# Loading the first two chunks of a windowed-attention kernel from two DMA queues instead of one

## Chip, cores and metric

The kernel runs on one core of a Trainium2 chip. The metric is the device time of one execution in microseconds (us). The kernel before took 175.13 and 176.15 us in two runs, with a median of 175.64 us. A lower time is better.

## What is computed

The input is four batches of eight heads, 768 tokens each, with 64 values per head. Each query sees the 128 tokens up to and including itself and, beyond these, the first four tokens of its batch (the sinks). The attention output goes through a feed-forward network with three first-layer matrices, of whose products the elementwise maximum is taken. The reference, cut to its core:

```python
scores = scale * np.matmul(q, k.transpose(0, 1, 3, 2))
is_sink = pos[None, :] < 4
rel = pos[:, None] - pos[None, :]
keep = is_sink | ((rel >= 0) & (rel < 128))
a = softmax(np.where(keep, scores, -1e9))
x = np.matmul(a, v)                      # to tokens x 512
h = np.maximum(np.maximum(x @ w1, x @ w2), x @ w3)
out = h @ w_out                          # 3072 x 512, float32
```

## The kernel before

**Tiling.** The 3072 tokens are cut into twelve chunks of 256 tokens (`ci` 0 to 11, three to a batch). For each chunk `load` (L93) brings Q, K and V of all eight heads from HBM as float32 tiles of 128 partitions by 8 heads by 2 tokens by 64 values, 512 KB each. With `parts=2` a load is cut by heads into two pieces of 256 KB: `part=0` holds heads 0 to 3 and `part=1` heads 4 to 7. An argument `gate` makes a small GpSimd instruction write into the tile first, so that the load waits for GpSimd; `eng` names the engine that issues the load, and is SyncE when it is left out.

**Stages of a chunk.** `cast_qk` (L112) turns half of the heads (`g` 0 or 1) of Q or K into bfloat16. `turn` (L132) and `turn2` (L156) transpose such a half with four TensorE matmuls against an identity into a PSUM tile `pt`, and copy that to `qT` or `kT`. `premask` (L306) writes an additive mask into the score tiles `st` with a matmul against the identity, `score` (L314) adds the products of `qT` and `kT` for the head pairs that it is given, `expo` (L392) takes the exponential on ScalarE into `e_sb`. Head half `g=1` serves pairs 2 and 3, half `g=0` pairs 0 and 1. `cast_v` (L121) turns V into bfloat16; `av` (L460) multiplies the probabilities with it into the tile `o`; `norm` (L478) divides, with a reciprocal and a multiplication on VectorE, into `x_sb`. `xpose` (L490) transposes `x_sb`, `ffn_h` (L511, matmuls on L524) makes the first layer with its maximum, `ffn_y` (L545) the second, `store` (L604) writes the result.

**The order of the work.** The schedule is written out by hand: each engine works through its instructions in the order in which the program text issues them to it, and waits only on semaphores for the data of others. Lines 191 to 265 set up constants; here ScalarE loads its activation table for the exponential (L194, by a first activation `one`), and VectorE zeroes the tile `wz`. From L639 on stands the start of the pipeline, call by call. `warm` (L198) issues matmuls of zeros whose result nobody reads: eight on L640 and four more on L650, between the transposes of Q's first half and the first mask. Since TensorE takes its instructions in order, whatever stands behind a warm call waits for it.

**Queues.** Before, every load of Q, K and V is issued by SyncE (SP), in the order: Q of chunk 0, heads 4 to 7 (L639); all of K (L641); Q, heads 0 to 3 (L642); V in two halves (L643, L645), the first of them gated by a GpSimd memset (L619); then K, Q and V of chunk 1 (L655, L663, L670). In the pages the transfers that SP or ScalarE issues are "hardware_dynamic" and show under one queue number. The weights are issued by GpSimd (`load_w`, L289), as "software_dynamic", each behind a cast on that engine that waits for an input: w1's columns 512 to 768 behind the cast of V of chunk 0, the next piece behind the cast of K of chunk 1, the third behind that of Q of chunk 1.

Of the kernel before, what the change touches and what calls it, by code (L numbers as in the profile page):

```python
# [16 lines left out]
def kernel(  # L17
# [13 lines left out]
    nc = tc.nc  # L31
# [17 lines left out]
    with tc.manual_schedule():  # L49
# [7 lines left out]
        def bank(shape, dtype, name):  # L57
            j = free.pop(0)
            x = psum.tile(shape, dtype, tag=f"b{j}", name=name)
            home[id(x)] = x, j  # L60
            return x
# [31 lines left out]
        def load(ci, what="kqv", gate=None, part=None, parts=1, eng=None):  # L93
            if ci >= NCH:
                return
            b, c = divmod(ci, CPB)
            t0 = c * 256
            for w in what:
                src = {"k": k, "q": q, "v": v}[w]
                if (ci, w) not in raws:  # L100
                    raws[ci, w] = raw.tile([128, H, 2, D], F32, tag=w + "_raw", name=w + "_raw")
                dst = raws[ci, w]
                if gate is not None:
                    gate(dst[0:1, 0, 0, 0:1])
                n = H // parts
                for g in range(parts) if part is None else (part,):
                    (eng or nc.sync).dma_start(
                        out=dst[:, n * g:n * g + n],
                        in_=src[b, n * g:n * g + n, t0:t0 + 256]
                            .rearrange("h (p i) d -> p h (i d)", i=2))  # L110

        def cast_qk(ci, w, g, eng):  # L112

            if (ci, w) not in bfs:
                bfs[ci, w] = raw.tile([128, NP, 2, 2, D], BF16, tag=w + "_bf", name=w + "_bf")
            x, y = bfs[ci, w], raws[ci, w]
            f = eng.copy if eng is nc.scalar else eng.tensor_copy
            f(x[:, 2 * g:2 * g + 2].rearrange("q p i a d -> q p a i d"),  # L118
              y[:, 4 * g:4 * g + 4].rearrange("q (p a) i d -> q p a i d", a=2))
# [12 lines left out]
        def turn(ci, w, g, eng=None):  # L132

            pt = bank([128, 4, 128], BF16, "pt")
            x = bfs[ci, w]
            for i in range(4):
                y = x[:, 2 * g + i // 2, i % 2]
                nc.tensor.transpose(pt[:, i], y.rearrange("s a d -> s (a d)"), ident)  # L138
            eng = eng or (nc.scalar if w == "q" else nc.vector)
            f = eng.copy if eng is nc.scalar else eng.tensor_copy  # L140
            if w == "q":
                f(
                    qT[ci % RING][:, 2 * g:2 * g + 2].rearrange("q p i n r -> q (p i) (n r)"), pt)
            elif ci >= NEW:
                f(
                    keys(ci)[:, 2 * g:2 * g + 2].rearrange("q p n h (i r) -> q p i (n h) r", i=2),
                    pt.rearrange("q (p i) (j r) -> q p i j r", p=2, j=4))
            else:
                f(
                    kT[ci % RING][:, :, 2 * g:2 * g + 2].rearrange("q n p i r -> q n (p i) r"),  # L150
                    pt.rearrange("q x (n r) -> q n x r", r=64))
            give(pt)
# [37 lines left out]

        wz = const.tile([128, 512], BF16, name="wz")
        nc.vector.memset(wz, 0.0)
        one = const.tile([128, 1], F32, name="one")
        nc.scalar.activation(one, wz[:, 0:1], AF.Exp)  # L194
        for x in vb:
# [2 lines left out]
        def warm(n):  # L198

            if n:  # L200
                pw = bank([128, 512], F32, "warm")
                for _ in range(n):
                    nc.tensor.matmul(pw, lhsT=wz[:, 0:128], rhs=wz, start=True, stop=True)  # L203
                give(pw)
# [14 lines left out]
        def masks():  # L219
            nc.gpsimd.memset(addm[:, 0:2], 0.0)  # L220
            for i in range(2):
                hp = slice(64 * i, 64 * i + 64)
                nc.gpsimd.affine_select(
                    out=addm[hp, 1], in_=addm[hp, 1], compare_op=ALU.is_ge, fill=NEG,
                    base=-i, pattern=[[1, 2], [2, 64]], channel_multiplier=-2)
                nc.gpsimd.affine_select(
                    out=addm[hp, 0], in_=addm[hp, 0], compare_op=ALU.is_gt, fill=NEG,
                    base=i, pattern=[[-1, 2], [-2, 64]], channel_multiplier=2)
            nc.vector.tensor_copy(addm0[:, 0], addm[:, 1])
            nc.vector.tensor_copy(addm0[:, 1], addm[:, 0])  # L230
            nc.vector.tensor_copy(addm0[:, 2], addm[:, 1])
            for i in range(2):
                nc.vector.memset(addm0[64 * i:64 * i + 2, 0:2], 0.0)
            nc.vector.tensor_copy(addm[:, 2:4], addm[:, 0:2])
# [71 lines left out]
        def premask(ci, pairs):  # L306
            lo = 0 if ci % CPB else 1
            for p in pairs:
                sts[ci, p] = [bank([128, 4, 128], F32, "st") for a in range(2)]
                for a in range(2):  # L310
                    nc.tensor.matmul(sts[ci, p][a][:, lo:], lhsT=ident, rhs=addm0 if lo else addm,  # L311
                                     start=True, stop=False, skip_group_check=True)
# [79 lines left out]
        def expo(ci, p):  # L392
            if ci >= NEW:
                return expo4(ci, p)
            lo = 0 if ci % CPB else 1
            e, st = es[ci, p]
            for a in range(2):
                nc.scalar.activation(e[:, a, lo:], st[a][:, lo:], AF.Exp, scale=scale)  # L398
                give(st[a])
# [238 lines left out]

        load(0, 'q', part=1, parts=2)  # L639
        warm(8)  # L640
        load(0, 'k')  # L641
        load(0, 'q', part=0, parts=2)  # L642
        load(0, 'v', part=0, parts=2, gate=pool_gate)  # L643
        cast_qk(0, 'q', 1, nc.scalar)
        load(0, 'v', part=1, parts=2)  # L645
        masks()
        sink_init()
        factors(msk, addm)
        turn(0, 'q', 1, nc.scalar)
        warm(4)  # L650
        premask(0, (2,))
        cast_qk(0, 'k', 0, nc.scalar)
        cast_qk(0, 'k', 1, nc.vector)
        turn(0, 'k', 1, nc.vector)
        load(1, 'k')  # L655
        turn(0, 'k', 0, nc.scalar)
# [3 lines left out]
        score(0, (3,))  # L660
        turn(0, 'q', 0, nc.vector)
        premask(0, (0,))
        load(1, 'q')  # L663
        expo(0, 2)
        cast_v(0, 1, 0, nc.gpsimd)
        cast_v(0, 0, 0, nc.vector)
# [333 lines left out]
```

## Time and profile before

| what | value |
|---|---|
| runs | 175.13 and 176.15 us, median 175.64 us |
| span of the profiled execution, first to last instruction | 173.5 us |
| median less that span | 2.14 us |
| TensorE busy, share of the span | 167.7 us, 97% |
| VectorE, ScalarE, GpSimd busy | 125.1, 88.8, 110.1 us |
| chain that ended last, by engine | TensorE 93%, VectorE 3%, ScalarE 1% |
| moved by DMA | 35.22 MB, mean 203 GB/s |

The profile is of one execution. Of that execution the page gives the span; what lies around it (start and end of the program) is taken as the difference to the median of the runs, 2.14 us. Engines are named PE (TensorE), PEld (its weight loads), DVE (VectorE), ACT (ScalarE), POOL (GpSimd) and SP (SyncE); a name with a q behind it is that engine's DMA queue. A row of the timeline holds the start and the duration in us, the engine, the line, the operation, what it writes and reads, and in brackets how long the engine had been idle and what released it. A row of the chain holds start, length and what stood in the chain.

### The profile page before, as it was taken

To read this page: it belongs to the slowest core of one execution; us is meant where nothing else is said; L and a number is where in the kernel's file an instruction comes from. 1 tells how busy PE (TensorE), PEld (TensorE's weight loads), DVE (VectorE), ACT (ScalarE), POOL (GpSimd) and SP (SyncE) were. 2 spreads that over 40 slices of the span, in tenths; PEclk is the share of its full clock that TensorE was granted. 3 is DMA by queue.
4 is the path that set the end of the run, shared out by engine and by line. 5 is a ranking of instruction groups with operands and counts; after the bars stand their busy time and mean duration, and the time that the engine had idled before them with its cause. 6 is when DMAs were issued, how large, how long until landed. Compare 5 with 4: busy or idle time off the path is not lost.

```text
span 173.5 us, 5418 instructions
## 1 busy us (share of the span) xinstructions
PE 167.7 (97%) x2225; PEld 129.2 (74%) x2225; DVE 125.1 (72%) x262; ACT 88.8 (51%) x183; POOL 110.1 (63%) x193
## 2 busy tenths in 40 slices
PE   7979999999999999999999999999999999999992
PEld 2546889857695697797797797797897896896871
DVE  3187856696697985986877977877778876776361
ACT  4598554587944615817726717627636516510210
POOL 7389507445399999999999999999998700000000
PEclk9999999999999999999999999999999999999999
DMA  4999999999996999988999969969999119017303
GB/s 134 300 289 198 216 217 252 219 274 290 292 210 118 250 264 180 252 188 220 264 186 247 264 165 254 257 163 238 257 176 274 32 34 376 21 35 272 121 2 121
DMA packets 71545, 35.22 MB, mean 203 GB/s; under 512 B 27488, under 2 KB 69984, under 8 KB 71520
## 3 DMA queue, kind: packets, MB, share of 16 engines
q1 hardware_dynamic: 65824, 31.60, 79.0%
q0 software_dynamic: 5552, 3.15, 12.8%
q8 instruction: 17, 0.28, 0.7%
q10 hardware_dynamic: 144, 0.13, 0.2%
q14 instruction: 8, 0.07, 0.1%
HBM read 25.17 MB, written 6.29 MB: 181 GB/s over the span
## 4 chain that ended last, share of the span: by engine, by line
PE 93%; DVE 3%; ACT 1%; issue 0%
PE h_ps L524 55%; PE y_ps L577 11%; PE y_ps L553 7%; PE o L471 7%; PE st L357 3%; PE warm L203 3%; PE st L331 3%; PE pt L138 2%; ACT e_sb L398 1%; PE o L453 1%; DVE x_sb L484 1%; PE sk L423 1%; PE y_ps L599 1%; DVE vb L123 1%; PE xt L496 1%; PE st L311 0%
## 5 line engine op out<-in xcount | busy, mean ns | idle before, releaser
L524 PE MATMUL h_ps<-xT,w 128*128 128x256 bf16 x864 | 101.2, 273 | 0.1
L524 PEld LDWEIGHTS <-w 128*128 128x128 bf16 x864 | 81.9, 98 | 9.9 <-issue 0.3
L540 DVE TENSOR_TENSOR h_sb<-h_sb,h_ps 128x512 bf16<-128x512 bf16 (+1 forms) x74 | 49.3, 671 | 20.0 <-PE h_ps L524 16.0
L536 ACT CAST h_sb<-h_ps 128x512 bf16<-128x512 f32 x35 | 20.5, 585 | 52.2 <-PE h_ps L524 52.2
L129 POOL CAST vb<-v_raw 32x512 bf16<-32x512 f32 x48 | 36.7, 764 | 2.8 <-DMA v_raw<-in_v_dram 0.6
L90 POOL CAST k_bf<-k_raw 32x512 bf16<-32x512 f32 x48 | 29.5, 614 | 2.2
L398 ACT ACTIVATE e_sb<-st 128x512 bf16<-128x512 f32 (+1 forms) x48 | 23.1, 588 | 0.7 <-PE st L331 0.7
L484 DVE TENSOR_TENSOR x_sb<-o,rc 128x256 bf16<-128x256 f32 x48 | 20.4, 424 | 1.6
L577 PE MATMUL y_ps<-wo,h_sb 64*64 64x512 bf16 (+1 forms) x312 | 21.1, 377 | 0.0
L471 PE MATMUL o<-vb,e_sb 128*128 128x65 bf16 x352 | 16.8, 193 | 0.4 <-ACT e_sb L398 0.4
L471 PEld LDWEIGHTS <-e_sb 128*128 128x128 bf16 x352 | 14.6, 97 | 2.8 <-issue 0.8
L123 POOL CAST vb<-v_raw 64x512 bf16<-64x512 f32 x18 | 12.4, 691 | 5.8 <-DMA v_raw<-in_v_dram 5.2
L389 DVE TENSOR_TENSOR e_sb<-e_part,msk 128x1024 bf16<-128x1024 bf16 x16 | 13.5, 865 | 3.1 <-ACT e_part L374 3.0
L406 DVE TENSOR_TENSOR e_sb<-e_sb,msk 128x1024 bf16<-128x1024 bf16 (+1 forms) x18 | 13.3, 756 | 2.1 <-ACT e_sb L398 2.0
L577 PEld LDWEIGHTS <-h_sb 64*64 64x64 bf16 (+1 forms) x312 | 9.9, 106 | 5.0
L374 ACT ACTIVATE e_part<-st 128x384 bf16<-128x384 f32 x32 | 13.1, 496 | 0.5 <-PE st L357 0.5
L553 PE MATMUL y_ps<-wo,h_sb 128*128 128x512 bf16 x54 | 13.0, 380 | 0.0
L481 DVE RECIPROCAL rc<-o 128x4 f32<-128x4 f32 x48 | 8.3, 174 | 3.5 <-PE o L471 3.4
L118 POOL CAST k_bf<-k_raw 128x512 bf16<-128x512 f32 x6 | 3.8, 647 | 9.6 <-DMA k_raw<-in_k_dram 9.4
L553 PEld LDWEIGHTS <-h_sb 128*128 128x128 bf16 x54 | 4.8, 97 | 5.6 <-DVE h_sb L540 0.9
L118 ACT CAST q_bf<-q_raw 128x512 bf16<-128x512 f32 x13 | 7.6, 621 | 2.0 <-DMA q_raw<-in_q_dram 1.9
L427 ACT ACTIVATE e_sink<-sk 128x256 bf16<-128x256 f32 x8 | 3.1, 389 | 10.0 <-PE sk L423 10.0
(90 smaller groups left out, 144.2 us busy)
## 6 DMA issues: line engine op xcount, KB each, us to landing
k_raw<-in_k_dram SPq DMA_DIRECT2D x11, 512.0 KB, 5.7
v_raw<-in_v_dram SPq DMA_DIRECT2D x11, 512.0 KB, 5.8
q_raw<-in_q_dram SPq DMA_DIRECT2D x10, 512.0 KB, 6.5
out_dram<-y_sb SPq DMA_DIRECT2D x9, 512.0 KB, 3.1
w<-in_moe_w_dram POOLq DMA_DIRECT2D x9, 256.0 KB, 6.6
q_raw<-in_q_dram SPq DMA_DIRECT2D x4, 256.0 KB, 7.7
out_dram<-y_sb SPq DMA_DIRECT2D x1, 1024.0 KB, 5.2
wo<-in_moe_w_out_dram POOLq DMA_DIRECT2D x2, 384.0 KB, 7.4
```

What stands on the lines that cost most here:

```text
L90: f(bfs[ci, "k"][x:x + 32, :, n], raws[ci, "k"][y:y + 32, :, i].rearrange("q (p a) d -> q p a d", a=2))
L123: eng.tensor_copy(vb[ci % RING][64 * i:64 * i + 64, n, :, 0:D], raws[ci, "v"][64 * n:64 * n + 64, :, i])
L129: eng.tensor_copy(vb[ci % RING][x:x + 32, n, :, 0:D], raws[ci, "v"][y:y + 32, :, i])
L389: nc.vector.tensor_mul(x.rearrange("q a (t s) c -> q (a t) s c", t=2), y, msk2)
L398: nc.scalar.activation(e[:, a, lo:], st[a][:, lo:], AF.Exp, scale=scale)
L471: nc.tensor.matmul(o[:, t, a], lhsT=e[:, a, s], rhs=vb[cv % RING][:, n, 2 * p + a], start=first, stop=True, skip_group_check=True)
L484: nc.vector.tensor_mul(xs[ci][:, p], o[:, :, :, 0:D], rc.unsqueeze(3).to_broadcast([128, 2, 2, D]))
L524: nc.tensor.matmul(hp[:, f].rearrange("q (i t r) -> q i t r", i=2, r=x.shape[3]), lhsT=w_sb[wi][:, ds, c0:c0 + 128], rhs=x, start=(ds == 0 ...
L536: (nc.scalar.copy if eng is nc.scalar else eng.tensor_copy)(dst, hp)
L540: nc.vector.tensor_max(dst[:, x], dst[:, x], hp[:, x])
L553: nc.tensor.matmul(yp, lhsT=hs[ci][:, fb, t * 128:(t + 1) * 128], rhs=wo[:, fb], start=(fb == 0), stop=(fb == FB - 1))
L577: nc.tensor.matmul(yps[ci][t][c:c + cols], lhsT=hs[ci][hp, fb, x:x + cols], rhs=wo[hp, fb], start=(turn == 0 and fb == 0), stop=(turn == 1 ...
```

## The change

K of chunk 0 is now loaded in two halves, and ScalarE issues them, with half of V, ahead of its table load; ScalarE also issues Q of chunk 1, behind its first cast. SyncE keeps both halves of Q and the other half of V of chunk 0, and K and V of chunk 1. Two casts of K that run on different engines change places in the text, which moves nothing on either engine.

```diff
         nc.vector.memset(wz, 0.0)
+        load(0, 'k', part=1, parts=2, eng=nc.scalar)
+        load(0, 'k', part=0, parts=2, eng=nc.scalar)
+        load(0, 'v', part=1, parts=2, eng=nc.scalar)
         one = const.tile([128, 1], F32, name="one")
         nc.scalar.activation(one, wz[:, 0:1], AF.Exp)
...
         load(0, 'q', part=1, parts=2)
         warm(8)
-        load(0, 'k')
         load(0, 'q', part=0, parts=2)
         load(0, 'v', part=0, parts=2, gate=pool_gate)
         cast_qk(0, 'q', 1, nc.scalar)
-        load(0, 'v', part=1, parts=2)
+        load(1, 'q', eng=nc.scalar)
...
+        cast_qk(0, 'k', 1, nc.vector)
         cast_qk(0, 'k', 0, nc.scalar)
-        cast_qk(0, 'k', 1, nc.vector)
...
         premask(0, (0,))
-        load(1, 'q')
         expo(0, 2)
```

SyncE's instructions at the start of the program, before. A tile of 128x4x128 is half of the heads, one of 128x8x128 all of them; the numbers behind the names tell chunk 0 (`q_raw_111`, `k_raw_122`, `v_raw_125`) from chunk 1 (`k_raw_181`, `q_raw_214`, `v_raw_223`).

```order
L107 DMA q_raw_111<-in_q_dram 128x4x128
L107 DMA k_raw_122<-in_k_dram 128x8x128
L107 DMA q_raw_111<-in_q_dram 128x4x128
L107 DMA v_raw_125<-in_v_dram 128x4x128 x2
L107 DMA k_raw_181<-in_k_dram 128x8x128
L107 DMA q_raw_214<-in_q_dram 128x8x128
L107 DMA v_raw_223<-in_v_dram 128x8x128
```

The same place now; chunk 0 is `q_raw_116` and `v_raw_90`, chunk 1 `k_raw_184` and `v_raw_224`, and `k_raw_382` is already chunk 2.

```order
L107 DMA q_raw_116<-in_q_dram 128x4x128 x2
L107 DMA v_raw_90<-in_v_dram 128x4x128
L107 DMA k_raw_184<-in_k_dram 128x8x128
L107 DMA v_raw_224<-in_v_dram 128x8x128
L107 DMA k_raw_382<-in_k_dram 128x4x128 x2
```

K of chunk 0, half of V and Q of chunk 1 have gone from this queue, so that K of chunk 1 now stands behind three pieces of 256 KB. The load of V of chunk 1 has a new wait there: it takes over the semaphore of the first half of K, and so waits until that has landed.

ScalarE's instructions at the start, before:

```order
L194 ACT_TABLE_LOAD
L194 ACTIVATE one_87<-wz_85 128x1
L118 CAST q_bf_128<-q_raw_111 128x2x2x2x64
L142 COPY qT0_73<-pt_157 128x512
L118 CAST k_bf_172<-k_raw_122 128x2x2x2x64
L149 COPY kT0_69<-pt_183 128x2x256
```

and now (every line behind L192 is three higher, so L197 is the old L194):

```order
L107 DMA k_raw_87<-in_k_dram 128x4x128 x2
L107 DMA v_raw_90<-in_v_dram 128x4x128
L197 ACT_TABLE_LOAD
L197 ACTIVATE one_92<-wz_85 128x1
L118 CAST q_bf_130<-q_raw_116 128x2x2x2x64
L107 DMA q_raw_132<-in_q_dram 128x8x128
L142 COPY qT0_73<-pt_160 128x512
L118 CAST k_bf_175<-k_raw_87 128x2x2x2x64
L149 COPY kT0_69<-pt_186 128x2x256
```

Three issues of 256 KB stand ahead of the table load, and one of 512 KB between the cast of Q's first half and the copy of its transpose. TensorE, VectorE and GpSimd have the same instructions in the same order as before.

## The prediction

> **What bounds the kernel now.** First I read the chain that ended last. TensorE holds 93% of it, and behind the first 16 us it is a row of matmuls without a gap:
>
> ```profile
> PE 93%; DVE 3%; ACT 1%; issue 0%
> 20.00:30.00 10.00, 10.00 (x106) 8.96 (x104) 6.05 (x13) 4.65 (x8) 2.99 (x5) 1.00 1.30 233
> ```
>
> The second row is of the view by stretches: 10.00 us of TensorE in 10.00. A delay of the start is therefore not made good later; it goes into the end one for one. What the change touches lies ahead of that, so next comes the chain in order of time over the start:
>
> ```profile
> 1.26 3.60 PE warm L203 x8
> 4.86 0.43 PE pt L138 x4
> 5.29 1.46 PE warm L203 x4
> 6.75 0.32 PE st L311 x2
> 7.07 0.45 PE pt L138 x8
> ...
> 7.84 0.35 PE st L331 x4
> 8.20 2.40 ACT e_sb L398 x6
> ...
> 12.21 0.33 DVE kT L171
> ...
> 13.63 0.33 DVE qT L168
> ...
> 15.88 1.03 PE h_ps L524 x8
> ```
>
> No transfer stands in it. From 1.26 to 8.20 us TensorE goes from the eight warm matmuls through Q's transposes (`pt`), four more warm ones, a mask, K's transposes and the first scores; then ScalarE's exponentials set the pace, then VectorE. So an earlier K buys nothing here: its transposes stand behind Q's and the warm matmuls. The timeline tells how near each transfer is:
>
> ```profile
> 3.99 0.62 ACT L118 CAST q_bf<-q_raw 128x512 bf16<-128x512 f32 x1 [1.68 <-DMA q_raw<-in_q_dram]
> 4.67 0.62 PE L138 MATMUL pt<-ident,q_bf 128*128 128x128 bf16 x4
> 5.32 0.59 ACT L142 COPY qT<-pt 128x512 bf16<-128x512 bf16 x1 [0.71 <-PE pt L138]
> 5.78 0.43 DVE L118 CAST k_bf<-k_raw 128x512 bf16<-128x512 f32 x1 [1.91 <-DMA k_raw<-in_k_dram]
> 6.58 0.49 PE L311 MATMUL st<-addm,ident 128*128 128x384 bf16 x2
> 6.91 0.61 PE L138 MATMUL pt<-ident,k_bf 128*128 128x128 bf16 x8
> ```
>
> Q's first half is cast from 3.99 to 4.61, and its transposes start at 4.67, with no idle time of TensorE before them: warm matmuls and cast end together. **Q's half has no slack.** K has some: VectorE's cast ends at 6.21, and K's transposes start at 6.91.
>
> **The first term: Q's half shares the engines.** Before, Q's half was alone at the head of the one queue. The list of issues gives its time to landing, and that of Q's second half:
>
> ```profile
> 0.81 0.46 SPq L107 DMA_DIRECT2D q_raw<-in_q_dram  x1
> q_raw<-in_q_dram SPq DMA_DIRECT2D x1, 256.0 KB, 3.2
> q_raw<-in_q_dram SPq DMA_DIRECT2D x1, 256.0 KB, 4.8
> ```
>
> It landed at 0.81 + 3.2 = 4.0. In the change ScalarE issues half of K at the same moment, since both engines leave the same barrier (ScalarE's first row of work started at 0.81 as well, below). How two queues share is seen where loads and weights are both under way, from 22 to 28 us, in packets, MB and share of the engines:
>
> ```profile
> q0 software_dynamic: 1282, 0.64, 77.2%
> q1 hardware_dynamic: 1269, 0.63, 52.0%
> ```
>
> They take turns, 1282 packets to 1269. And the sixteen DMA engines have no room for a second stream: the stretches (the last two columns are their busy share and GB/s) are
>
> ```profile
> 2.20:3.20 1.00, 1.00 (x4) 0.35 (x3) 0.54 (x3) 0.11 (x1) 0.83 (x5) 1.00 0.74 219
> 3.20:4.00 0.80, 0.80 (x3) 0.30 (x2) 0.56 (x4) 0.01 (x1) 0.58 (x5) 1.00 0.98 286
> 4.00:5.00 1.00, 1.00 (x7) 0.34 (x5) 0.00 (x0) 0.61 (x1) 0.94 (x2) 1.00 1.12 331
> 5.00:6.00 1.00, 1.00 (x6) 0.45 (x5) 0.22 (x1) 0.68 (x2) 0.25 (x1) 1.00 1.17 303
> ```
>
> One queue alone fills them from about 3.2 us. Now the arithmetic. A half is 262 KB. With some 20 KB moved by 2.2 us (an estimate from the ramp), 219 + 20 = 239 KB are there by 3.2, and Q's half is complete 23 KB later, at 3.28; it landed at 4.0, so 0.7 us pass between last byte and landing. If the halves of Q and K come in turn, both are complete at 524 KB: 239 + 0.8 x 286 = 468 KB at 4.0, and 56 KB at 331 GB/s more is 4.17. Both land at about 4.9. That is 0.9 later for Q, 0.9 earlier for K's first half (the cast of K started at 5.78), and since Q has no slack, **0.9 us** goes into the path: cast 4.9 to 5.5, transposes at 5.6 instead of 4.67, and the four warm matmuls, the mask and all behind them as much later. The bounds: 0 if SyncE's ring is served first; if ScalarE's three pieces are all served first, Q's half is complete at 1049 KB, where before the second half of Q was (issued at 1.87 with 4.8 to landing, so 6.7): 2.7. I take the even share, which the packets show.
>
> The Trainium skill, "DMA: Bandwidth & Descriptors", section "Issuing engines are not separate DMA queues", speaks against the change: queues of different issuing engines end on the same sixteen DMA engines, and a second issuer saves issue time only. The trace agrees as far as it goes (1282 to 1269 packets, and a share of 1.17 by one queue). By that rule the term comes out as the same 0.9.
>
> **The second term: ScalarE's own time.** Its table load now stands behind three issues:
>
> ```profile
> 0.81 1.28 ACT L194 ACT_TABLE_LOAD   x1 [0.81 <-PEq L981]
> 1.87 0.57 SPq L107 DMA_DIRECT2D q_raw<-in_q_dram  x1
> 4.00 0.73 SPq L107 DMA_DIRECT2D k_raw<-in_k_dram  x1
> 4.77 1.71 SPq L107 DMA_DIRECT2D q_raw<-in_q_dram  x1
> ```
>
> A 256 KB issue took 0.46 to 0.57 us on SyncE. Three of them at 0.57 end at 2.5, table load and `one` (1.28 + 0.20) at 4.0, ahead of Q's landing at 4.9: **0**. If two issuers slow each other to twice that, it is 5.7, which is 0.8 more. Then Q of chunk 1, 512 KB, is issued behind the cast that ends at 5.5. SyncE took 0.73 for one such load, and 1.71 for the next, when 2 MB had been issued ahead of it; ScalarE's queue has then had 0.75 MB, half of it moved, so I take 0.73: done at 6.25. The copy of Q's transposes starts 0.65 behind their start (5.32 less 4.67), which is 6.25: **0**. At 1.71 the copy ends at 7.8, and K's second cast 8.4; TensorE reaches its transposes at 8.05, so this bound costs 0.4. K's second half, which lands at 6.6 with Q's, is cast by ScalarE from 6.9 to 7.5, ahead of 8.05: **0**. Its lateness (some 0.9 behind the old landing of K) is covered by the delay that Q makes; without that delay it would itself cost some 0.3.
>
> **The third term: chunk 1.** K of chunk 1 stood ahead of Q of chunk 1 in one queue; now both run side by side and complete together, at what was Q's place.
>
> ```profile
> k_raw<-in_k_dram SPq DMA_DIRECT2D x1, 512.0 KB, 6.3
> q_raw<-in_q_dram SPq DMA_DIRECT2D x1, 512.0 KB, 7.3
> 10.39 0.60 POOL L118 CAST k_bf<-k_raw 128x512 bf16<-128x512 f32 x1
> 12.12 0.61 POOL L118 CAST q_bf<-q_raw 128x512 bf16<-128x512 f32 x1 [0.43 <-DMA q_raw<-in_q_dram]
> 12.13 0.42 DVE L171 COPY kT<-pt 128x512 bf16<-128x512 bf16 x1
> ```
>
> Landings before: K at 4.00 + 6.3 = 10.3, Q at 4.77 + 7.3 = 12.1. Now both at about 11.9. GpSimd's cast of K goes from 10.4 to 11.9 to 12.5; its transposes take 0.40, so the copy `kT` could start at 13.0. VectorE, 0.9 late, comes to it at 12.13 + 0.9 = 13.0: **0 to 0.2**, I take 0.1. Behind that cast on GpSimd stand a weight issue (0.75) and the cast of Q of chunk 1, at 13.2 instead of 12.12, which is 1.1 later; VectorE wants its transposes 0.9 later, and it had some 0.4 of room (cast done at 12.73, transposes at 13.2, copy `qT` in the chain at 13.63). V of chunk 1 waits for K's first half at 4.9 before it is issued; behind K of chunk 1 that is early enough. The weights move only when the loads are through: from 9.2 to 13 us their queue has
>
> ```profile
> q0 software_dynamic: 15, 0.01, 1.5%
> ```
>
> 15 packets. The loads' bytes are the same, so the weights come no later than before.
>
> The sum is 0.9 + 0 + 0.1 = **1.0 us later**. On the span of the profiled execution, 173.5 us, that gives 174.5; with the 2.14 us that lie between that span and the median of the runs, **176.6 us**, against 175.64. Within the bounds of the single terms it is 176.0 to 177.4.
>
> **The rivals.**
>
> *Not slower: SyncE's ring goes ahead.* If SyncE's descriptors enter the engines first and ScalarE's only fill behind them, Q's half lands at 4.0 as before, and the chain starts at the old times. What speaks for it: a newcomer did wait where a queue was already deep (the weights' 15 packets). Against it: here both start empty. It decides from the point where Q's half lands by 4.1. K's second half would then cost up to 0.3, and as nothing in the chain waits for a transfer there is nothing to win: 175.5 to 175.9, say 175.7. Chance 0.25.
>
> *Slower by more: the gap keeps TensorE slow.* The single warm matmuls show two paces:
>
> ```profile
> 5.08 0.63 PE L203 MATMUL warm<-wz 128*128 128x512 bf16 x1
> 6.36 0.39 PE L203 MATMUL warm<-wz 128*128 128x512 bf16 x1
> ```
>
> Up to 5.93 they follow each other in 0.43 us, and from 6.36 on a matmul takes about half, after 5.1 us without a pause. The granted clock in the view is 1.00 throughout, so this is not in that column. With Q at 4.9 TensorE pauses from 4.66 to 5.6. If the count starts anew there, TensorE reaches its full pace only near 5.6 + 5.1 = 10.7. The pieces from 6.75 to 8.20, 1.45 us, would then take 2.9, and of the 2.4 us under the exponentials a part more: 1.45 plus at most 1.2 on top of 1.0, so 178.1 to 179.3. If the full pace comes half-way, it is about 177.9, which I take for the case. Chance 0.2. The Trainium skill, "TensorE: Matmul & The Clock Gate", section "What's actually happening", says that the array's clock is released by activity over a free-running window of about 3.4 us, so that the moment shifts from run to run; by it a pause of 0.9 may or may not spoil one window, which the one trace here cannot tell.
>
> *The issue of Q of chunk 1 holds ScalarE* for 1.71 us, or two issuers slow each other: 1.0 + 0.4 or 0.8, 177.0 to 177.4. Chance 0.05.
>
> **How the numbers follow.** The forecast has 0.5, the rivals 0.25, 0.2 and 0.05. The range goes from the low end of the first rival less the noise between runs to the upper part of the second: 175.2 to 178.4. A measurement of this kernel tells about 2% from no change, which is 3.5 us: slower by over 2% starts at 179.15 and needs the clock's worst case, 0.05; for faster by over 2% the profile offers no mechanism, 0.01; 0.94 remains.
>
> **What would show it.** In the changed profile the first cast of ScalarE should start near 4.9, the idle time before it be put down to the transfer of Q, TensorE stand idle for some 0.9 us ahead of Q's transposes, the cast of K on VectorE come ahead of 5.3, and GpSimd's cast of K of chunk 1 be released by its transfer near 11.9; the first L524 row, at 15.88 in the chain before, should start near 16.9. A first cast at 4.0 shows the first rival; transposes of K 0.11 apart behind 7.5 show the second. If the first L524 row starts ahead of 15.9, the reading that no transfer bounds the start is wrong.

## The result, and the profile after

The changed kernel took 178.29 and 178.44 us, median 178.37, against 175.64 before: a ratio of 1.016 (95% interval 1.0123 to 1.0196). It is slower by 2.7 us. The forecast was 176.6, slower by 1.0: the direction was right, and the size was out by 1.8 us; the time lies just inside the upper end of the range. The profiled execution took 178.44 us, with a span of 176.7 (173.5 before).

The chain of waits of the changed kernel, its shares by engine and its first pieces:

```profile
PE 78%; DMA 12%; POOL 5%; issue 1%; SPq 1%; DVE 0%; POOLq 0%; DVEq 0%
2.42 8.69 DMA k_raw<-in_k_dram
12.53 1.49 issue
14.05 0.62 POOL q_bf L118
15.96 1.43 POOL w L295 x2
19.61 1.64 POOL w L295 x3
21.25 12.68 DMA q_raw<-in_q_dram
```

Before, no transfer stood in this chain, and TensorE held 93% of it. Now transfers hold 12% and GpSimd 5%: K of chunk 1, GpSimd's cast of Q of chunk 1, the weight issues behind that cast, and a load of chunk 2. The loss thus reaches beyond the first ten microseconds. The timeline of the changed kernel shows the start:

```profile
4.86 0.62 ACT L118 CAST q_bf<-q_raw 128x512 bf16<-128x512 f32 x1 [0.85 <-DMA q_raw<-in_q_dram]
4.87 0.38 ACTq L107 DMA_DIRECT2D q_raw<-in_q_dram  x1
5.32 0.43 DVE L118 CAST k_bf<-k_raw 128x512 bf16<-128x512 f32 x1 [1.44 <-DMA k_raw<-in_k_dram]
5.54 0.40 PE L138 MATMUL pt<-ident,q_bf 128*128 128x128 bf16 x4 [0.94 <-ACT q_bf L118]
5.77 1.03 PE L206 MATMUL warm<-wz 128*128 128x512 bf16 x4
6.96 0.39 PE L138 MATMUL pt<-ident,k_bf 128*128 128x128 bf16 x4
7.12 0.62 ACT L118 CAST k_bf<-k_raw 128x512 bf16<-128x512 f32 x1 [0.56 <-DMA k_raw<-in_k_dram]
7.79 0.40 PE L138 MATMUL pt<-ident,k_bf 128*128 128x128 bf16 x4 [0.44 <-ACT k_bf L118]
8.81 3.17 ACT L401 ACTIVATE e_sb<-st 128x384 bf16<-128x384 f32 x8
```

Q's first half is cast at 4.86 instead of 3.99, and its transposes start at 5.54 instead of 4.67. The four warm matmuls then take 1.03 us, where they took 1.67 before, because TensorE had reached its full pace earlier in this execution; so K's first transposes start at 6.96, only 0.05 later. What is late next is K's second half: its cast starts at 7.12, its transposes at 7.79, and the exponentials at 8.81 instead of 8.20. **The start costs 0.6 us.** The larger part comes with chunk 1:

```profile
11.24 0.60 POOL L118 CAST k_bf<-k_raw 128x512 bf16<-128x512 f32 x1 [0.31 <-DMA k_raw<-in_k_dram]
14.05 0.62 POOL L118 CAST q_bf<-q_raw 128x512 bf16<-128x512 f32 x1 [1.51 <-DMA q_raw<-in_q_dram]
14.72 0.40 PE L164 MATMUL pt<-ident,q_bf 128*128 128x128 bf16 x4 [1.17 <-POOL q_bf L118]
17.49 1.03 PE L527 MATMUL h_ps<-xT,w 128*128 128x256 bf16 x8
19.61 0.92 SPq L107 DMA_DIRECT2D k_raw<-in_k_dram  x2
19.93 1.03 PE L527 MATMUL h_ps<-xT,w 128*128 128x256 bf16 x8
```

The rows of before for the last two of these are

```profile
17.59 0.92 SPq L107 DMA_DIRECT2D k_raw<-in_k_dram  x2
18.02 1.04 PE L524 MATMUL h_ps<-xT,w 128*128 128x256 bf16 x8
```

GpSimd's cast of Q of chunk 1 waits for its transfer until 14.05, where it started at 12.12 before. TensorE stands idle for 1.17 us ahead of its transposes. The first two groups of L527 (the old L524), which were at 15.88 and 18.02, are at 17.49 and 19.93, so 1.6 and then **1.9 us late**. GpSimd issues the weights behind that cast, and behind the weights it opens the gate for the loads of chunk 2; SyncE issues these at 19.61, where it was 17.59 before. The list of issues gives the time from issue to landing of Q of chunk 1, and the view of the queues shows the packets from 8 to 9 us:

```profile
q_raw<-in_q_dram ACTq DMA_DIRECT2D x1, 512.0 KB, 9.1
q1 hardware_dynamic: 536, 0.27, 109.3%
q10 hardware_dynamic: 34, 0.02, 6.5%
```

q1 is SyncE's queue and q10 ScalarE's: they show under two numbers, not under one as said above. Q of chunk 1 was issued at 4.87 and needed 9.1 us (7.3 before); from 8 to 9 us ScalarE's queue, in which it stood, moved 34 packets to SyncE's 536. Last, the last group of 72 in the chain, before and after:

```profile
159.67 7.86 PE h_ps L524 x72
```

```profile
162.49 7.86 PE h_ps L527 x72
```

It is 2.82 us late: 0.6 in the start, 1.3 more by 20 us, and 0.9 after that. The spans of the two profiled executions differ by 0.4 more, behind the last matmul.

### The profile page after: what moved, and what is told of

It reads as the page before. It is cut to its first block, busy times and chain, and to the rows that moved or that the text cites. A ratio compares the mean times of both kernels' runs of the same rounds, so it can differ in the third digit from the quotient of the medians.

```text
span 176.7 us, 5418 instructions
## 1 busy us (share of the span) xinstructions
PE 167.9 (95%) x2225; PEld 128.5 (73%) x2225; DVE 124.8 (71%) x262; ACT 88.9 (50%) x183; POOL 110.2 (62%) x193
## 4 chain that ended last, share of the span: by engine, by line
PE 78%; DMA 12%; POOL 5%; issue 1%; SPq 1%; DVE 0%; POOLq 0%; DVEq 0%
PE h_ps L527 46%; PE y_ps L580 10%; DMA q_raw<-in_q_dram 7%; PE y_ps L556 7%; PE o L474 6%; DMA k_raw<-in_k_dram 5%; PE st L360 3%; POOL w L295 3%; PE st L334 2%; PE o L456 1%; SPq L107 1%; PE y_ps L602 1%; PE pt L138 1%; POOL vb L123 1%; PE sk L426 1%
## 5 line engine op out<-in xcount | busy, mean ns | idle before, releaser
L527 PE MATMUL h_ps<-xT,w 128*128 128x256 bf16 x864 | 101.2, 273 | 0.0
L527 PEld LDWEIGHTS <-w 128*128 128x128 bf16 x864 | 81.8, 98 | 10.0 <-DVE q_bf L118 0.2
L409 DVE TENSOR_TENSOR e_sb<-e_sb,msk 128x1024 bf16<-128x1024 bf16 (+1 forms) x18 | 13.9, 800 | 2.3 <-ACT e_sb L401 2.3
L392 DVE TENSOR_TENSOR e_sb<-e_part,msk 128x1024 bf16<-128x1024 bf16 x16 | 12.9, 814 | 3.4 <-ACT e_part L377 3.1
```

The costliest lines, as they stand in the source:

```text
L409: (eng or nc.vector).tensor_mul(e[:, :, lo:], e[:, :, lo:], msk0[0] if lo else msk)
L527: nc.tensor.matmul(hp[:, f].rearrange("q (i t r) -> q i t r", i=2, r=x.shape[3]), lhsT=w_sb[wi][:, ds, c0:c0 + 128], rhs=x, start=(ds == 0 ...
```

## The experiments

Each kernel was compared with the kernel before on the same chip, in five rounds. The first four ran together, then four, then two; the medians of before were 175.37, 175.64 and 175.52 us. The theory at the outset: the time lies in Q of chunk 1, which as a newcomer in the second queue waits behind what was issued before it, and in the weight issues that wait for its cast.

**Q of chunk 1 back on SyncE.** The change, with this load between K and V of chunk 1 again:

```diff
         cast_qk(0, 'q', 1, nc.scalar)
-        load(1, 'q', eng=nc.scalar)
...
         premask(0, (0,))
+        load(1, 'q')
```

> The change, but Q of chunk 1 is issued by SyncE again, between K and V of chunk 1. My theory now: most of the loss comes from Q of chunk 1 landing at 14.0 us instead of 12.1, because ScalarE's queue stood empty-handed from 8.0 to 9.5 us and then shared with V of chunk 1. Then Q of chunk 1 lands near 12.1 here, the first L524 matmul stands near 16.5 (17.49 in the change, 15.88 before), and only the delay of the start, about 0.6 us, is left: 176.0 to 176.7 us. Rival: the loss comes from the shared start (halves of Q and K of chunk 0 side by side) and is carried on; then it stays at 177.5 to 178.5 us.

It took 176.38 us, ratio 1.0063 (1.0037 to 1.0089). Its timeline, and the last line of its chain:

```profile
12.21 0.62 POOL L118 CAST q_bf<-q_raw 128x512 bf16<-128x512 f32 x1
16.45 1.03 PE L527 MATMUL h_ps<-xT,w 128*128 128x256 bf16 x8
```

```profile
160.44 7.86 PE h_ps L527 x72
```

The cast is at 12.21, no longer released by a transfer, and the first L527 group 0.57 later than before instead of 1.61. By the ratios (1.016 and 1.0063) 1.7 us of the loss hang on where this one load is issued, by the last group 2.05; the rest of the change costs about 1 us.

**That load alone on ScalarE.** The kernel before, with only this load moved:

```diff
         load(0, 'v', part=1, parts=2)
+        load(1, 'q', eng=nc.scalar)
...
         premask(0, (0,))
-        load(1, 'q')
```

> The kernel before, with one part of the change alone: Q of chunk 1 issued by ScalarE behind its first cast. Theory: a load on a second queue gets no turn while the first queue is deep, so its first packets come 3 us or more after its issue near 4.0 us, and it lands after 12.1 us, perhaps near 12.8; time 176.2 to 177.2 us. Rival: queues take even turns from the issue on; then Q of chunk 1 lands near 8.5 to 9.5 us, and V of chunk 0, which now shares, near 10 instead of 8.6, so that the first products with V start later.

It took 178.37 us, ratio 1.0175 (1.0139 to 1.0211): this one line costs as much as the whole change. But neither expectation described it. Its timeline, the packets from 8 to 9 us, and a row of the stretches:

```profile
3.87 0.45 ACTq L107 DMA_DIRECT2D q_raw<-in_q_dram  x1
12.21 0.60 POOL L118 CAST k_bf<-k_raw 128x512 bf16<-128x512 f32 x1 [1.66 <-DMA k_raw<-in_k_dram]
12.87 0.61 PE L164 MATMUL pt<-ident,k_bf 128*128 128x128 bf16 x4 [1.98 <-POOL k_bf L118]
```

```profile
q10 hardware_dynamic: 546, 0.28, 111.0%
q1 hardware_dynamic: 20, 0.01, 4.4%
```

```profile
13.00:14.00 1.00, 1.00 (x14) 1.00 (x13) 0.49 (x2) 0.24 (x1) 1.00 (x2) 0.50 1.43 199
```

Here Q of chunk 1 went ahead, not behind: with 546 packets to 20 it had the engines almost alone, and landed at 10.8 (issued at 3.87, 6.9 to landing), while K of chunk 1, whose issue on SyncE ran from 3.84 to 4.86, landed at 12.1 instead of 10.3. The missing load was then K: TensorE idled 1.98 us, and from 13 us its granted clock is 0.50 (the number behind GpSimd's busy time). So the loss here is not the loss of the change over again: all six executions show a mean granted clock of 0.981 to 0.996, the change's two 0.997 and 1.00. My theory of a newcomer that always waits fell. What fits both kernels is **service in the order of issue, across both queues**. In the changed kernel 2.1 MB had been issued ahead of Q of chunk 1; adding up that kernel's GB/s stretch by stretch, they are through at 9.6, and its queue, silent from 8.6 us on, comes up between 9.2 and 9.6. In this kernel 1.57 MB stood ahead; they are through near 7.5, and its first 30 packets come from 7.2 to 7.4. What counts cannot be the moment at which the issue starts, since Q and K of chunk 1 started theirs within 0.03 us here and did not share; SyncE's issue, behind a deep queue, took 1.02 us and ended 0.54 later than ScalarE's. That the end decides is an inference that no run tests.

**That load issued early.** The change, with Q of chunk 1 issued by ScalarE right behind its half of V, at 2.51:

```diff
         load(0, 'v', part=1, parts=2, eng=nc.scalar)
+        load(1, 'q', eng=nc.scalar)
...
-        load(1, 'q', eng=nc.scalar)
         masks()
```

> The change, but ScalarE issues Q of chunk 1 right behind its half of V, ahead of the table load, instead of behind the first cast. Theory: Q's late landing comes from its late issue into a queue pair that is already deep. Issued early, its packets follow the half of V without a gap, it lands near 12.0 us, the first L524 matmul stands near 16.5 and the time is 176.0 to 176.8 us. Rival: ScalarE's queue simply gets less, or sharing with V of chunk 1 alone makes Q late; then Q lands at 13.5 to 14 and the time stays at 177.8 to 178.5 us.

It took 177.58 us, ratio 1.0121 (1.0085 to 1.0156), 0.8 above what I expected. From its timeline and its stretches:

```profile
12.33 0.60 POOL L118 CAST k_bf<-k_raw 128x512 bf16<-128x512 f32 x1 [1.35 <-DMA k_raw<-in_k_dram]
12.83 0.62 ACT L118 CAST q_bf<-q_raw 128x512 bf16<-128x512 f32 x1
```

```profile
13.00:14.00 1.00, 1.00 (x13) 1.00 (x14) 0.36 (x2) 0.45 (x1) 1.00 (x2) 0.50 1.42 214
```

Now K (issued at 2.42) and Q (2.51) of chunk 1 share evenly, 1249 to 1050 packets from 8 to 12 us, and land at 12.2 and 12.8. Q is 1.2 us ahead of its landing in the change, though 0.8 behind what I expected, and K is late: its cast waits for its transfer until 12.33, TensorE idles 1.12 us and its clock falls to 0.50. This profiled execution took 178.46; the three with a mean granted clock of 1.00 took 176.68 to 177.09, so part of the loss comes only with the drop of the clock. This is the layout of the prediction's third term, side by side and landing close together; that term gave it 0.1 us.

**The cut of K by itself.** The kernel before, one queue, with K of chunk 0 in two loads; run twice, and the casts exchanged as in the change:

```diff
-        load(0, 'k')
+        load(0, 'k', part=1, parts=2)
+        load(0, 'k', part=0, parts=2)
```

> The kernel before with K of chunk 0 cut in two halves, all loads still on SyncE in the old order. Theory: VectorE's cast of K starts near 5.0 instead of 5.78 us, but K's transposes stay at 6.9 because they stand behind Q's transposes and the warm matmuls, and the time does not move: 175.3 to 175.9 us, an interval that holds 1.0. Rival: K's landing does bound the start, and an earlier first half gains 0.5 us or more.

> The kernel before with K of chunk 0 cut in two halves on one queue, once more, for a second profile. The first time it was 1.6 us slower where no difference was expected, and the DMA engines, which moved 300 to 340 GB/s from 2.7 us on, fell to 135 to 160 GB/s from 4.2 to 5.0 us, so that V of chunk 0 landed 0.6 us late. Theory: the cut itself makes that dip, and it shows again between 4 and 5 us, with a time of 176.2 to 177.4 us. Rival: the dip was chance; then there is none, V's first cast on GpSimd starts near 8.6 us and the time is within 0.4 us of the kernel before.

176.96 us, ratio 1.0091 (1.0062 to 1.0121), and again 177.04, ratio 1.0077 (1.0037 to 1.0118). From the first one's stretches and timeline:

```profile
4.00:5.00 1.00, 1.00 (x7) 0.38 (x5) 0.23 (x1) 0.57 (x1) 0.94 (x2) 1.00 0.63 169
```

```profile
5.08 1.91 PE L203 MATMUL warm<-wz 128*128 128x512 bf16 x4
6.42 0.62 ACT L118 CAST k_bf<-k_raw 128x512 bf16<-128x512 f32 x1 [0.52 <-DMA k_raw<-in_k_dram]
9.25 0.61 POOL L123 CAST vb<-v_raw 64x512 bf16<-64x512 f32 x1 [1.29 <-DMA v_raw<-in_v_dram]
```

The cut alone costs 1.4 to 1.6 us. From 4 to 5 us the engines move 169 GB/s, and 223 in the second run, where it was 331 before; K's second half comes at 6.42 (K whole was there at 5.78) and V at 9.25 instead of 8.61. So the 1 us that is left with Q of chunk 1 back on SyncE needn't come from the two queues at all. Why the transfers slacken there is open, and that they make the whole loss is not shown: in both profiles TensorE was also slow for all four warm matmuls (1.91 us for 1.67), which by itself puts K's transposes 0.3 us later, and the last group is 0.5 us late in the first profiled execution (176.10, the fastest of its six) and 1.15 in the second (176.76).

**K whole on ScalarE.** The kernel before, with K of chunk 0 in one piece on ScalarE's queue:

```diff
+        load(0, 'k', eng=nc.scalar)
         one = const.tile([128, 1], F32, name="one")
...
-        load(0, 'k')
```

> The kernel before with one part of the change: K of chunk 0 issued by ScalarE ahead of its table load, but whole, 512 KB; V and Q of both chunks stay with SyncE. Theory: the shared start costs what it did with Q of chunk 1 back on SyncE; Q's first half lands at 4.4 to 4.9 us and the time is 0.5 to 1.1 us above the kernel before. Rival: it is the cut of K into two loads that costs, as on one queue; then this one stays within 0.3 us of the kernel before.

176.10 us, ratio 1.0034 (0.9986 to 1.0083), from 175.37 to 177.51: not told apart from no change, and so it settles nothing between the cut and the sharing. Its profiled execution was one of the longest, 177.47, and shows one way in which they scatter:

```profile
7.74 0.85 PE L312 MATMUL st<-addm,ident 128*128 128x384 bf16 x2
8.38 1.06 PE L138 MATMUL pt<-ident,k_bf 128*128 128x128 bf16 x8
```

Q's half came at 4.96, TensorE idled 0.78 us ahead of its transposes, and then went on at the slow pace: the mask 0.85 us (0.49 before), K's eight transposes 1.06 (0.61). That is the prediction's second rival, in this execution though not in that of the changed kernel.

**The weights ahead of the late cast.** The change, with the two weight loads that stand behind GpSimd's cast of Q of chunk 1 moved ahead of it:

```diff
+        load_w(0, 0, 256)
+        load_w(1, 512, 768)
         cast_qk(1, 'q', 0, nc.gpsimd)
         cast_qk(1, 'q', 1, nc.scalar)
         turn(1, 'k', 1, nc.scalar)
-        load_w(0, 0, 256)
...
-        load_w(1, 512, 768)
```

> The change, with GpSimd issuing two more pieces of the weights (the third of w1 and the first of w2) ahead of its cast of Q of chunk 1 instead of behind it. In the change the feed-forward block is 1.9 us late at its start and 2.8 us late at its end; the DMA engines were half idle between 16 and 20 us, because the weights' issues stood behind that cast. Theory: the weights, pushed back, run into the loads of chunk 2 and cost the further 0.9 us; here these loads get the engines back, GpSimd's cast of K of chunk 2 (29.63 us in the change, 26.87 before) comes at least 0.8 us earlier, and the time is 177.4 to 178.0 us. Rival: chunk 2 is late only because its own issue on SyncE is gated 2 us late; then nothing changes, 178.1 to 178.7 us.

177.36 us, ratio 1.0094 (1.0059 to 1.0129). Its timeline and chain:

```profile
13.98 0.64 POOL L118 CAST q_bf<-q_raw 128x512 bf16<-128x512 f32 x1
17.50 1.03 PE L527 MATMUL h_ps<-xT,w 128*128 128x256 bf16 x8
18.11 1.61 SPq L107 DMA_DIRECT2D k_raw<-in_k_dram  x2
```

```profile
161.41 7.86 PE h_ps L527 x72
```

Q of chunk 1 and the first L527 are as late as in the change, chunk 2's loads are issued 1.5 us earlier, and the last group comes 1.08 us earlier. That is the last 0.9 us of the account: it is the weights behind the cast and the loads behind the weights, not the cast itself. The weights and chunk 2's loads moved together here, so what share each has is not shown.

**V of chunk 1 out of the way.** The change, with V of chunk 1 gated behind GpSimd's cast of Q's second half, so that it is issued at 6.92 instead of 5.31:

```diff
         cast_qk(0, 'q', 0, nc.gpsimd)
+        load(1, 'v', gate=pool_gate)
...
-        load(1, 'v')
```

> The change, but SyncE's load of V of chunk 1 is gated behind GpSimd's cast of Q's second half, so that it is issued near 7.2 instead of 5.3 us. Theory: both queues together are served about in the order of issue; Q of chunk 1 was late because it was issued only 0.4 us ahead of V of chunk 1 and shared every turn with it. Here it has the engines to itself behind K, lands at 12.2 to 12.7 us, the first L524 matmul stands at 16.4 to 16.9, and the time is 176.2 to 177.0 us. Rival: ScalarE's queue lost its place by running empty at 8 us and is held back by SyncE's queue whatever stands there; then Q lands after 13.3 us and the time is 177.6 us or more.

176.96 us, ratio 1.0072 (1.0034 to 1.011). Its timeline, and the packets from 10 to 11 us:

```profile
12.35 0.62 POOL L118 CAST q_bf<-q_raw 128x512 bf16<-128x512 f32 x1
16.59 1.03 PE L527 MATMUL h_ps<-xT,w 128*128 128x256 bf16 x8
```

```profile
q10 hardware_dynamic: 560, 0.29, 114.5%
q1 hardware_dynamic: 9, 0.00, 1.3%
```

With V issued 2.3 us behind it, Q of chunk 1 (issued at 4.63) has the engines to itself, 560 packets to 9, and its cast starts at 12.35, as it did before the change within 0.3. So in the change it was late because it shared with V of chunk 1, issued 0.4 us behind it; by the ratios that is worth 1.5 us. In the profiled execution about 1 us was lost again behind 20 us: its chain goes through V of chunk 2, which came at 35.1 (32.6 before, 35.7 in the change), to an idle time of TensorE of 0.49 us near 41. Why V came so late I don't know.

**Both corrections, and the weights alone.** The gate and the weights together; and the kernel before with the weights moved:

> The change with both corrections at once: V of chunk 1 gated behind GpSimd's cast of Q of chunk 0 (its load is issued near 6.9), and two weight loads issued ahead of GpSimd's cast of Q of chunk 1 instead of behind it. Theory (the loss is three separate pieces: the start some 0.6 to 0.8 us, the late landing of Q of chunk 1 some 1.3, the weights pushed back behind its cast some 0.9): with Q of chunk 1 back at 12.3 the two weight loads gain only the 1 us that they stand ahead of the cast, so most of what they can give has been given by the gate: first L527 row at 16.5 to 16.7, last x72 block at 160.6 to 161.3, 176.3 to 176.9 us, 0.1 to 0.6 below the gate alone (176.96). Rival (the two corrections act on two unconnected losses and add): 178.37 less 1.4 less 1.0, 175.7 to 176.1 us, x72 at 159.9 to 160.4.

> The kernel before with the two weight loads issued ahead of GpSimd's cast of Q of chunk 1. Theory (before, the weights came in time, since GpSimd's cast of Q of chunk 1 started at 12.12 with only 0.43 us of waiting, and TensorE has no gap behind 16 us): no difference, 175.3 to 175.9 us, last x72 block within 0.3 of 159.67; the cast itself may come 0.3 to 1.1 later, since two issues of 0.75 us stand ahead of it, which would then cost up to 0.7. Rival (the early weights save time in this kernel whatever the loads do): faster by 0.5 to 1.0, 174.6 to 175.1 us.

Together 177.07 us, ratio 1.0088 (1.0061 to 1.0115): no better than the gate alone, and 0.2 above what the theory gave. The weights alone, in the kernel before: 176.28 us, ratio 1.0048 (1.0027 to 1.007), slower, as the condition at the end of that expectation had it. The timeline of the first, and timeline and chain of the second:

```profile
13.62 0.64 POOL L118 CAST q_bf<-q_raw 128x512 bf16<-128x512 f32 x1
```

```profile
13.27 0.64 POOL L118 CAST q_bf<-q_raw 128x512 bf16<-128x512 f32 x1
13.97 0.40 PE L164 MATMUL pt<-ident,q_bf 128*128 128x128 bf16 x4 [1.37 <-POOL q_bf L118]
```

```profile
160.72 7.86 PE h_ps L524 x72
```

No transfer holds these casts now; the two weight issues ahead of them do. The second kernel gives the price of a late cast: with the loads of Q, K and V where they were before and the weights early, the cast starts 1.15 us late and the last group 1.05 us late (0.8 us by the ratio). What corrects the changed kernel thus does harm where Q comes in time. No version that was run beats the kernel before.

## Why the prediction was wrong, step by step

**No transfer in the chain, and TensorE carries a delay to the end: right, but not one for one.** The weights alone come near it (1.15 in, 1.05 out). In the change 1.9 us at 20 us were 2.8 at the end, since more work stood behind the late cast. The 2.14 us between span and time mix two executions: where both are known for the same one, the time is 1.7 us above the span (178.44 against 176.7). The term stands in the time before as well as in the forecast, so the difference of 1.0 doesn't hang on it.

**First term, Q's first half shares (0.9): right at its place, in part by luck, and carried to 0.6.** Cast 4.86 (4.9 forecast), transposes 0.87 later. But from 2.2 to 3.2 us the engines moved 129 GB/s where the working had 219, and the halves did not land together: K's was cast at 5.32, since SyncE's queue sent 160 packets from 2.2 to 3 us and ScalarE's 19. A slower start and a larger share for Q seem to have nearly cancelled. The delay was not carried as the step had it: K's first transposes came almost in time, since TensorE was fast earlier, and the wait then stood at K's second half, at 7.1 where the working had 6.6. And the cut of K, which the sum carried at nothing, came with 1.4 to 1.6 us even on one queue with Q's half at 3.96. What share of the start is the sharing's and what the cut's, these runs don't separate.

**Second term, ScalarE's own time (0): right for the issues.** Table load and `one` hid behind the wait for Q, and the issue of Q of chunk 1 took 0.38 us behind the cast. K's second half was not hidden, as just said.

**Third term, chunk 1 (0.1): this is the step that failed.** It said that K and Q of chunk 1 "run side by side and complete together, at what was Q's place", 11.9 for both. They did not: K landed at 11.1 and Q at 14.0. The step let two queues share evenly whatever had been issued when, from a row on loads and weights (1282 to 1269), not on two queues of loads. What fits the runs is service of both queues about in the order of issue, and only loads issued close together share: Q, issued at 4.87, stood behind K (2.42) and beside V (5.31), which the step had called "early enough" without asking with whom it shares. In place of 0.1 that measured 1.3 of the 2.7 us. And where the layout of the step did occur, with the load issued early, it cost 1.2 us more than the same kernel with that load on SyncE (177.58 against 176.38, on one chip), and 0.3 to 0.7 in the executions whose clock did not fall, so 0.1 was wrong for that too: the step asked only when VectorE would come to the copy of K's transposes, and not what stands behind these on TensorE, nor what its clock does in the gap.

**"The weights come no later than before": wrong,** by 0.9 us. The step counted the bytes of the loads and not the order on GpSimd: the issues stand behind the cast that waits, and the gate of chunk 2 stands behind the issues. Moving them ahead, and chunk 2's gate with them, gave 1.0 us back.

**The rivals.** SyncE's queue went ahead only for the first packets (160 to 19), and Q's half still landed at 4.86. TensorE kept its pace in the changed kernel's profiled execution, so the clock rival's 177.9, near the measured time, was near it for another reason; its mechanism, a slow pace behind the gap at the start, showed only with K whole on ScalarE. The issue on ScalarE held nothing.

The Trainium skill, "DMA: Bandwidth & Descriptors", section "Queues, rings and completion order", says that a DMA engine takes turns, packet by packet, between the queues for which it has work. Between the weights and the loads this held in the prediction's row (1282 to 1269). Between SyncE's and ScalarE's queues it held where the loads had been issued close together (1249 to 1050). Elsewhere the packets were 536 to 34, 20 to 546 and 9 to 560 in 1 us, with loads issued and not yet landed on both sides. For loads that have been issued the measurement decides; whether the engines already had the work of the silent queue is not shown by any run.

## What to carry to other kernels

A second issuing queue gave no more transfer rate here once the engines were full; it only changed whose turn it was, and a load moved to it took its place about by its moment of issue. So list all loads by that moment, across queues, add up the bytes ahead of each and ask which will share with it, before asking what is early enough. Then follow the engine that waits for the late one: what it issues behind that wait is late too, and here it cost half as much again (0.9 us behind 1.9).

## What the hardware showed beyond that

- *A start from two queues.* From 2.2 to 3.2 us the engines moved 105 to 157 GB/s in the seven kernels that load from both queues at the start, and 219 to 276 in the five that start from one. By 4 us the changed kernel had moved some 60 KB less than the kernel before, an estimate from these rates.
- *Alternation by issue.* In the changed kernel the queue with the most packets changes with each microsecond: ScalarE's 416 to 174 from 5 to 6 us, SyncE's 412 to 171, ScalarE's 385 to 205, SyncE's 536 to 34 from 8 to 9.
- *A cut load.* Two loads of 256 KB instead of one of 512 KB in the same queue went with a rate of 169 and 223 GB/s from 4 to 5 us, in both profiles, in place of 331.
- *TensorE's clock.* With idle times of 1.98 us and 1.12 us it was granted 0.50 for some 3.4 us, an estimate from the means of the stretches (Q of chunk 1 alone on ScalarE, and issued early); with the 1.17 us in the changed kernel and the 1.37 in the kernel before with the weights moved it stayed at 1.00, so the length of the pause alone does not decide. The moment at which the start reaches full pace moved, though the first warm matmul always started near 1.26: 4.2 us in the changed kernel and in the one with the weights moved, 6.4 before, behind 6.7 with K cut on one queue, between 9.2 and 10.5 with K whole on ScalarE. The Trainium skill, "TensorE: Matmul & The Clock Gate", section "What's actually happening", puts that down to an activity window that runs freely; the spread here is wider than the half microsecond either way that it gives.
